# Turning q and k by crossbar DMA transposes instead of PE transposes, in a fused attention and SwiGLU kernel

## The chip, the cores and the metric

One core of a Trainium2 chip. The metric is the time of one execution on the device in microseconds (us), lower is better.

The engines are named as in the profile: PE (TensorE, matmuls), PEld (its weight loads), DVE (VectorE), ACT (ScalarE), POOL (GpSimd), SP (the sync queue, which only issues DMAs). PSUM is the memory that matmuls write to.

## The reference

Eight batches of attention with eight heads, 576 positions and head size 64, with a decay from f; its output (4608 tokens of 512) is normalised and goes through a SwiGLU layer of width 1536.

```python
scores = q @ k.T / sqrt(64) + cum[:, None] - cum[None, :]   # cum = cumsum(log f), causal
x   = softmax(scores) @ v                                   # 4608 x 512 over all heads
xn  = x / sqrt(mean(x * x) + 1e-6) * rms_g
out = (silu(xn @ w_gate) * (xn @ w_val)) @ w_out
```

## The kernel before

All is in bf16 on PE. The kernel emits attention of batch 0, then interleaves the attention of the batches 1 to 7 with the feed-forward work of nine output groups of 512 tokens. A scheduler of the framework sets the final order of instructions on each engine, and each engine works through its own list in order.

```python
qb = [ldp.tile([128, NB, H * D], BF16, name=f"qb{i}") for i in range(2)]   # two buffers
kb = [ldp.tile([128, NB, H * D], BF16, name=f"kb{i}") for i in range(2)]
Vs = [ldp.tile([128, NB, H, D + 1], BF16, name=f"Vs{i}") for i in range(2)]
def load_qk(b):                                   # POOL issues, casts to bf16
    for j in range(NB):
        for src, dst in ((q, qb[b % 2]), (k, kb[b % 2])):
            nc.gpsimd.dma_start(out=dst[0:n, j, :]..., in_=src[b, :, p0:p0 + n, :]...)
def load_v(b):                                    # the sync queue issues
    ...  nc.sync.dma_start(out=v32[0:n, :, :], in_=v[b, ...]...)
# ... weights are loaded in pieces by POOL ...
def scale_v(b):                                   # "Vs": POOL, ten instructions a batch
    for j in range(NB):
        nc.gpsimd.tensor_tensor(Vs[b % 2][0:n, j, :, 0:D], v32[0:n, :, :], bcast(dj, D), ALU.mult)
        nc.gpsimd.tensor_copy(Vs[b % 2][0:n, j, :, D], dj)
def transposes(b, p):                             # four head pairs p
    for src, store, nm in ((qb[b % 2], QT, "QT"), (kb[b % 2], KT, "KT")):
        tp = ps_tr.tile([128, NB * 128], BF16, name="tr")
        for j in range(NB):
            nc.tensor.transpose(tp[:, j * 128:(j + 1) * 128], src[:, j, p * 128:(p + 1) * 128], ident)
        t = store[b, p] = qkt.tile([128, NB * 128], BF16, name=f"{nm}{p}")
        nc.vector.tensor_copy(t, tp)
# scores (PE, exp on ACT, causal mask on POOL), values (PE, scaled on DVE) ...
def norm(b):
    ...                                           # squares on ACT
    nc.gpsimd.tensor_scalar(ms, in0=sq, ...)      # POOL
    nc.gpsimd.tensor_tensor(rs, ms, mhalf, ALU.pow)
    for j in range(NB):
        nc.vector.tensor_scalar_mul(xn[:, j, :], x[:, j, :], rs[:, j:j + 1])   # DVE
# transpose_x(b): PE turns xn for the feed-forward part ...
for i in range(3): load_w(i)
load_qk(1); load_v(1); load_wo()
for _, work in attention(0): work()
for b in range(1, B):
    stream.append((0.0, lambda b=b: (load_qk(b + 1), load_v(b + 1)) if b + 1 < B else None))
    stream += attention(b)        # transposes, last score rows and scale_v, scores, values, norm, transpose_x
# ... stream is dealt out between the pieces of the feed-forward work ...
```

POOL issues the q and k loads, scales v (Vs), masks the scores, and makes rs, the factor of the norm.

The softmax here doesn't subtract the row's maximum and nothing guards it: scores larger than these inputs give would overflow.

Of the kernel before, what the change touches and what calls it, by code (L numbers as in the profile page):

```python
# [9 lines left out]
BF16 = mybir.dt.bfloat16  # L10
# [13 lines left out]
def kernel(  # L24
# [12 lines left out]
    nc = tc.nc  # L37
    B, H, S, D = q.shape
    assert (B, H, S, D) == (8, 8, 576, 64)
    BH = B * H  # L40
    NB = 5
# [9 lines left out]
    ldp = ctx.enter_context(tc.tile_pool(name="ldp", bufs=1))  # L51
    vp = ctx.enter_context(tc.tile_pool(name="vp", bufs=6))
    qkt = ctx.enter_context(tc.tile_pool(name="qkt", bufs=2))
# [7 lines left out]
    ps_tr = ctx.enter_context(tc.tile_pool(name="ps_tr", bufs=1, space=PSUM))  # L61
# [5 lines left out]
    qb = [ldp.tile([128, NB, H * D], BF16, name=f"qb{i}") for i in range(2)]  # L67
    kb = [ldp.tile([128, NB, H * D], BF16, name=f"kb{i}") for i in range(2)]
    Vs = [ldp.tile([128, NB, H, D + 1], BF16, name=f"Vs{i}") for i in range(2)]
    PT4 = [[ldp.tile([128, 5 * 64], BF16, name=f"PT4_{i}{j}") for j in range(2)] for i in range(2)]  # L70


    def load_qk(b):
        for j in range(NB):
            p0, n = j * 128, min(128, S - j * 128)
            for src, dst in ((q, qb[b % 2]), (k, kb[b % 2])):
                nc.gpsimd.dma_start(  # L77
                    out=dst[0:n, j, :].rearrange("p (h d) -> p h d", d=D),
                    in_=src[b, :, p0:p0 + n, :].rearrange("h p d -> p h d"))
# [10 lines left out]
    fr = consts.tile([BH, S], F32)  # L90
    nc.sync.dma_start(out=fr, in_=f.rearrange("b h s -> (b h) s"))

    for t in qb + kb:
        nc.vector.memset(t[64:128, NB - 1, :], 0.0)
    load_qk(0)
    load_v(0)
    for t in Vs:
        nc.vector.memset(t[64:128, NB - 1, :, :], 0.0)
    for pair in PT4:
        for t in pair:  # L100
# [4 lines left out]
    ident = consts.tile([128, 128], BF16)  # L105
# [46 lines left out]
    QT, KT, PT = {}, {}, {}  # L152
# [8 lines left out]
            nc.gpsimd.tensor_copy(Vs[b % 2][0:n, j, :, D], dj)  # L161

    def transposes(b, p):
        for src, store, nm in ((qb[b % 2], QT, "QT"), (kb[b % 2], KT, "KT")):
            tp = ps_tr.tile([128, NB * 128], BF16, name="tr")
            for j in range(NB):
                nc.tensor.transpose(tp[:, j * 128:(j + 1) * 128], src[:, j, p * 128:(p + 1) * 128], ident)  # L167
            t = store[b, p] = qkt.tile([128, NB * 128], BF16, name=f"{nm}{p}")
            nc.vector.tensor_copy(t, tp)

    def scores4(b):

        for par in range(2):
            sc = ps_sc.tile([128, 512], F32, name="sc")
            rows = slice(par * 64, par * 64 + 64)
            for p in range(4):
                nc.tensor.matmul(sc[:, p * 64:(p + 1) * 64], lhsT=KT[b, p][rows, 512:640],
                                 rhs=QT[b, p][rows, 512:576], start=True, stop=True)
            t = PT4[b % 2][par]
            nc.scalar.activation(t[:, 0:256], sc[:, 0:256], ACT.Exp, scale=scale)  # L180
# [35 lines left out]
    def weights_of(b, h, qi, kj):  # L216
        if qi == 4:
            if kj == 4:
                c = (h // 2) * 64
                return PT4[b % 2][h % 2][:, c:c + 128]  # L220
            return PT[b, h][:, 1024 + kj * 64:1024 + kj * 64 + 128]
# [47 lines left out]
    def attention(b):  # L269

        a = []
        for p in range(4):
            a.append((0.6, lambda p=p: transposes(b, p)))
        a.append((0.2, lambda: (scores4(b), scale_v(b))))
        for p in range(4):
            for bank in range(3):
                a.append((0.35, lambda p=p, bank=bank: scores(b, p, bank)))
                if p > 0 and bank > 0:
                    a.append((0.45, lambda h=2 * (p - 1) + bank - 1: values(b, h)))
        a.append((0.45, lambda: values(b, 6)))  # L280
        a.append((0.45, lambda: values(b, 7)))
        a.append((0.0, lambda: norm(b)))
        for dc in range(NDC):
            a.append((0.3, lambda dc=dc: transpose_x(b, dc)))
        return a
# [53 lines left out]
    done_a, i, n = 0.0, 0, 0  # L339
# [40 lines left out]
```

## Time and profile before

486.84 us, median of two runs (486.47 to 487.2). The profiled execution spans 484.0 us.

From the page of the kernel before: the busy time of each engine, and the span in 40 equal slices of 12.1 us (a digit is a share in tenths, 9 is 90% or more; PEclk is the clock granted to PE; DMA is the mean share of the 16 DMA engines; in the tables of windows it adds up the times of all packets, which overlap, so it can exceed 1).

```profile
span 484.0 us, 8505 instructions
...
PE 423.9 (88%) x3317; PEld 207.6 (43%) x3317; DVE 260.3 (54%) x534; ACT 222.1 (46%) x436; POOL 187.7 (39%) x335
...
PE   0491707999999999999999999999999999999996
...
PEclk9999999999999999999999999999999999999999
DMA  9999991594190419041903290010001000201102
```

From the eighth slice on PE is busy 90% or more of every slice but the last. Before that it mostly is not, and in the first six of those slices the DMA engines are full. The table of windows says the same of two stretches, the start and one batch in the middle (busy us and number of instructions by engine, the granted clock, the DMA share and rate):

```profile
core 0: us, PE busy (x) PEld busy (x) DVE busy (x) ACT busy (x) POOL busy (x), PEclk, DMA share, GB/s
0.00:72.00 72.00, 28.03 (x237) 15.67 (x237) 15.75 (x47) 21.26 (x40) 56.13 (x94) 1.00 1.51 180
192.00:240.00 48.00, 46.83 (x398) 22.97 (x396) 29.49 (x62) 26.02 (x52) 22.60 (x40) 1.00 0.57 73
```

A batch in the middle takes 48.0 us, PE is busy 46.83 of them, so PE sets the pace there. The timeline of PE shows how a batch hands over to the next (start, duration, engine, line, operation; in brackets the idle time before and what ended it):

```profile
214.21 0.23 PE L258 MATMUL tr<-ident,xn 128*128 128x128 bf16 x1 [0.96 <-DVE xn L252]
...
220.85 0.44 PE L167 MATMUL tr<-ident,qb_100 128*128 128x128 bf16 x5
221.12 0.81 PE L311 MATMUL ff<-wo,hT 128*128 128x512 bf16 x3
```

PE waits 0.96 us for the normalised x. Line 167 is the transposes that the change takes away, here of the next batch, between matmuls of the feed-forward part. Each group of five covers 0.44 us.

The rs of norm 0 begins at 70.09 us.

### The profile page before, as it was taken

The page shows a single profiled execution, that of the slowest core. Times are in us where ns is not written, and L with a number is a line of the kernel's source. Part 1 is how long each engine was busy: PE and PEld are TensorE (multiplying, and loading weights), DVE is VectorE, ACT ScalarE, POOL GpSimd, SP SyncE. Part 2 cuts the span into 40 slices and gives each one's busy share as a digit, 9 for nine tenths or more (in the row PEclk, how much of TensorE's full clock was granted, in tenths as well). Part 3 has the DMA queues.
Part 4 walks back from the last instruction along what each step waited for, and adds up shares of the span by engine and source line. Part 5 has one row for each costly group of instructions (what it writes and reads, how often), then busy time and mean ns, then how long its engine had stood idle before and what let it go on. Part 6 is the DMA issues. An engine that isn't in the chain of part 4 may idle for free.

```text
span 484.0 us, 8505 instructions
## 1 busy us (share of the span) xinstructions
PE 423.9 (88%) x3317; PEld 207.6 (43%) x3317; DVE 260.3 (54%) x534; ACT 222.1 (46%) x436; POOL 187.7 (39%) x335
## 2 busy tenths in 40 slices
PE   0491707999999999999999999999999999999996
PEld 0231403454544454445444544454444544444442
DVE  3210326478447844784478457745774577373670
ACT  3060321664465437544754474447444744232321
POOL 8539990665182518252825282513111211000000
PEclk9999999999999999999999999999999999999999
DMA  9999991594190419041903290010001000201102
GB/s 151 175 195 178 191 187 33 36 65 99 65 120 3 100 66 119 3 100 67 120 1 77 70 118 0 1 66 23 3 0 66 23 1 0 88 1 45 43 1 87
DMA packets 123080, 33.73 MB, mean 70 GB/s; under 512 B 113760, under 2 KB 118368, under 8 KB 123040
## 3 DMA queue, kind: packets, MB, share of 16 engines
q0 software_dynamic: 79744, 14.16, 36.6%
q1 hardware_dynamic: 43296, 19.03, 14.9%
q8 instruction: 26, 0.43, 0.4%
q14 instruction: 14, 0.11, 0.1%
HBM read 37.90 MB, written 9.44 MB: 98 GB/s over the span
## 4 chain that ended last, share of the span: by engine, by line
PE 67%; POOL 13%; issue 6%; DMA 6%; ACT 5%; DVE 2%; POOLq 0%; ACTq 0%
PE ff L311 20%; PE ff L296 14%; PE ff L304 13%; PE sc L202 7%; PE po L231 5%; PE tr L167 4%; DMA wv<-in_moe_w_val_dram 3%; PE tr L258 3%; POOL Vs_104 L160 2%; DMA qb_100<-in_q_dram 2%; ACT junk L245 2%; POOL Vs_105 L160 2%; POOL rs L249 2%; ACT PT L205 2%; POOL qb_100 L77 2%
## 5 line engine op out<-in xcount | busy, mean ns | idle before, releaser
L205 ACT ACTIVATE PT<-sc 128x512 bf16<-128x512 f32 x192 | 105.1, 599 | 87.6 <-PE sc L202 73.8
L296 PE MATMUL ff<-xT,wg 128*128 128x512 bf16 x432 | 114.7, 382 | 0.7 <-DVE xT L265 0.6
L304 PE MATMUL ff<-xT,wv 128*128 128x512 bf16 x432 | 114.0, 380 | 0.0
L311 PE MATMUL ff<-wo,hT 128*128 128x512 bf16 x432 | 112.5, 380 | 0.0
L301 DVE SCALAR_TENSOR_TENSOR ga<-th,ff 128x512 f32<-128x512 f32 x108 | 74.2, 687 | 66.9 <-ACT th L299 66.3
L299 ACT ACTIVATE th<-ff 128x512 f32<-128x512 f32 x108 | 64.5, 598 | 82.6 <-PE ff L296 80.9
L306 DVE SCALAR_TENSOR_TENSOR hT<-ga,ff 128x512 bf16<-128x512 f32 x108 | 74.2, 687 | 9.0 <-PE ff L304 0.3
L304 PEld LDWEIGHTS <-wv 128*128 128x128 bf16 x432 | 42.2, 98 | 50.2 <-issue 2.5
L208 POOL TENSOR_SCALAR_AFFINE_SELECT PT<-PT 128x128 bf16<-128x128 bf16 x64 | 19.1, 299 | 97.8 <-ACT PT L205 97.6
L296 PEld LDWEIGHTS <-wg 128*128 128x128 bf16 x432 | 38.6, 98 | 42.0 <-issue 5.6
L314 ACT COPY ores<-ff 128x512 f32<-128x512 f32 x36 | 21.1, 586 | 75.2 <-PE ff L311 74.4
L213 POOL TENSOR_SCALAR_AFFINE_SELECT PT<-PT 128x384 bf16<-128x384 bf16 x64 | 33.0, 528 | 53.2 <-ACT PT L205 53.1
L311 PEld LDWEIGHTS <-hT 128*128 128x128 bf16 x432 | 36.5, 98 | 36.4 <-issue 9.5
L231 PEld LDWEIGHTS <-PT 128*128 128x128 bf16 x896 | 35.7, 102 | 31.2 <-POOL PT L208 9.7
L234 DVE RECIPROCAL rden<-po 128x5 f32<-128x5 f32 x64 | 12.2, 191 | 55.3 <-PE po L231 55.3
L258 PE MATMUL tr<-ident,xn 128*128 128x128 bf16 x160 | 20.6, 229 | 18.3 <-DVE xn L252 18.0
L231 PE MATMUL po<-Vs_104,PT 128*128 128x65 bf16 x448 | 22.7, 206 | 13.6 <-POOL PT L208 9.2
L235 DVE TENSOR_TENSOR x<-po,rden 128x320 f32<-128x320 f32 x64 | 31.4, 490 | 1.7
L245 ACT ACTIVATE junk<-x 128x512 bf16<-128x512 f32 x40 | 25.0, 624 | 9.0 <-DVE x L235 8.4
L258 PEld LDWEIGHTS <-xn 128*128 128x128 bf16 x160 | 12.4, 100 | 37.0 <-DVE xn L252 29.1
L265 DVE TENSOR_SCALAR xT<-tr,rg 128x512 bf16<-128x512 bf16 (+7 forms) x64 | 20.5, 362 | 12.3 <-PE tr L258 12.1
L252 DVE TENSOR_SCALAR xn<-x,rs 128x512 bf16<-128x512 f32 x40 | 18.1, 520 | 13.2 <-POOL rs L249 13.2
(300 smaller groups left out, 387.8 us busy)
## 6 DMA issues: line engine op xcount, KB each, us to landing
out_dram<-ores SPq DMA_DIRECT2D x36, 256.0 KB, 2.0
qb_100<-in_q_dram POOLq DMA_DIRECT2D x16, 128.0 KB, 5.3
kb_102<-in_k_dram POOLq DMA_DIRECT2D x16, 128.0 KB, 5.4
qb_101<-in_q_dram POOLq DMA_DIRECT2D x16, 128.0 KB, 4.4
kb_103<-in_k_dram POOLq DMA_DIRECT2D x16, 128.0 KB, 4.5
wg<-in_moe_w_gate_dram POOLq DMA_DIRECT2D x3, 512.0 KB, 12.7
wv<-in_moe_w_val_dram POOLq DMA_DIRECT2D x3, 512.0 KB, 14.0
wo<-in_moe_w_out_dram POOLq DMA_DIRECT2D x2, 768.0 KB, 12.3
```

The costliest lines, as they stand in the source:

```text
L202: nc.tensor.matmul(sc[:, c:c + n], lhsT=KT[b, p][rows, kj * 128:(kj + 1) * 128], rhs=QT[b, p][rows, q0:q0 + n], start=True, stop=True)
L205: nc.scalar.activation(t[:, bank * 512:(bank + 1) * 512], sc, ACT.Exp, scale=scale)
L213: nc.gpsimd.affine_select(out=d, in_=d, pattern=[[0, 3], [1, 128]], compare_op=ALU.is_ge, fill=0.0, base=0, channel_multiplier=-1)
L231: nc.tensor.matmul(po[:, qi, :], lhsT=weights_of(b, h, qi, kj), rhs=Vs[b % 2][:, kj, h, :], start=(kj == 0), stop=(kj == qi))
L245: nc.scalar.activation(junk, x[:, j, :], ACT.Square, accum_out=sq[:, j:j + 1])
L258: nc.tensor.transpose(tp[:, j * 128:(j + 1) * 128], xn[:, j, dc * 128:(dc + 1) * 128], ident)
L296: nc.tensor.matmul(pg, lhsT=wg[:, dc, fc * 128:(fc + 1) * 128], rhs=xT[:, dc, :], start=(dc == 0), stop=(dc == NDC - 1))
L299: nc.scalar.activation(t, pg, ACT.Tanh, scale=0.5)
L301: nc.vector.scalar_tensor_tensor(a, in0=t, scalar=1.0, in1=pg, op0=ALU.add, op1=ALU.mult)
L304: nc.tensor.matmul(pv, lhsT=wv[:, dc, fc * 128:(fc + 1) * 128], rhs=xT[:, dc, :], start=(dc == 0), stop=(dc == NDC - 1))
L306: nc.vector.scalar_tensor_tensor(hTs[g][:, fc, :], in0=a, scalar=0.5, in1=pv, op0=ALU.mult, op1=ALU.mult)
L311: nc.tensor.matmul(po, lhsT=hTs[g][:, fc, j * 128:(j + 1) * 128], rhs=wo[:, fc, :], start=(fc == 0), stop=(fc == NFC - 1))
```

## The change

The intent is to take 320 transposes with their weight loads off PE, the engine that sets the pace, and 64 copies out of PSUM off DVE. Ten DMA transposes a batch, from SBUF to SBUF on the sync queue, turn whole rows of heads (128 x 512, the last one 64 x 512).

```diff
+    QTs = [ldp.tile([128, 4, NB * 128], BF16, name=f"QTs{i}") for i in range(2)]
+    KTs = [ldp.tile([128, 4, NB * 128], BF16, name=f"KTs{i}") for i in range(2)]
 ...
-    for t in qb + kb:
-        nc.vector.memset(t[64:128, NB - 1, :], 0.0)
+    for t in QTs + KTs:
+        nc.vector.memset(t[:, :, S:], 0.0)
 ...
     def transposes(b, p):
-        for src, store, nm in ((qb[b % 2], QT, "QT"), (kb[b % 2], KT, "KT")):
-            tp = ps_tr.tile([128, NB * 128], BF16, name="tr")
+        if p > 0:
+            return
+        for src, store, ts in ((qb[b % 2], QT, QTs), (kb[b % 2], KT, KTs)):
+            t = ts[b % 2]
             for j in range(NB):
-                nc.tensor.transpose(tp[:, j * 128:(j + 1) * 128], src[:, j, p * 128:(p + 1) * 128], ident)
-            t = store[b, p] = qkt.tile([128, NB * 128], BF16, name=f"{nm}{p}")
-            nc.vector.tensor_copy(t, tp)
+                n = min(128, S - j * 128)
+                nc.sync.dma_start_transpose(out=t[:, :, j * 128:j * 128 + n], in_=src[0:n, j, :])
+            for pp in range(4):
+                store[b, pp] = t[:, pp, :]
```

## The prediction

> **What bounds the kernel now.** The page gives a span of 484.0 us with PE busy 423.9 (88%). Busy time by stages: from 144 to 384 us every 48.0 us are one batch, PE busy 46.8 of them, DVE 29.5, ACT 26.0, DMA share 0.5 falling to 0.06. There PE's in-order stream is the bound. From 0 to 72 us it is not: PE is busy 28 us, the DMA share is above 1 at 155 to 191 GB/s, and the chain of waits runs through q/k loads, weight loads and POOL (Vs scaling from 40.4, norm at 70).
>
> **What goes.** 320 PE transposes with weight loads, and 64 DVE copies of 128x640 out of PSUM (492 ns each, 31 us, DVE not the bound). In the timeline five pipelined transposes show as 0.44 us but push PE's next matmul back only 0.27 to 0.37. Eight groups a batch: 2.2 to 3.0 us; over the seven batches after the first, 15 to 21 us. The chain of waits agrees (line 167: 3.6% of the span, 17.4 us). All of it is on the critical path.
>
> **What comes.** 80 crossbar transposes of 128x512 (64x512) bf16 on the sync queue, ten a batch[...]. The trace has no such operation. The Trainium skill (VectorE: DVE Perf Modes, The three transpose paths) gives 1309 ns for 128x128 by DMA; four blocks in series would be 5.2 us. Its page DMA: Bandwidth & Descriptors (Latency and other measured facts) has 261 GB/s for one kernel, 0.5 us per 128 KB. My estimate lies between: 1 to 2.5 us each in throughput, 3 to 5 us to landing. Ten are 10 to 25 us of DMA per 45 us of PE: it fits beside a share of 0.5.
>
> **Is it on the path?** By the order of instructions the sync queue takes the transposes of a batch well ahead of its scores (those of batch 4 stand after the first output group, their scores two groups later), so in steady state a landing of 10 us is hidden. Stores and v loads share the queue but have slack. Expected: 45.0 to 45.8 us a batch.
>
> The start differs. The first ten transposes wait for q and k (last near 19.5 us), then issue into saturated DMA engines, where sync issues took 2.2 us each and v loads 6 to 10 us to land. First scores move from 22.7 to about 30 to 36 us. Much is hidden, since values wait for POOL's Vs (46 us) anyway; but weight loads and POOL's queue slip. Against that, the new order lets PE do much of batch 1's scores and values before the first norm, in its idle stretch from 60 to 72. I net these at -4 to +12 us.
>
> **Prediction:** 486.8 - 18 - 1 = about 468 us, 8 in 10 between 454 and 498. Chances: faster 0.62, same 0.22, slower 0.16.
>
> **Signs.** Right: a batch period of 45 to 46 us with PE 97% busy; median landing of a transpose under 6 us; no wait of scores on a DMA after 100 us; first scores near 33 us. Wrong at the start: first scores after 40 us, norm of batch 0 after 80. Wrong in steady state: scores waiting on transposes, or sync-queue waits in front of v loads.
>
> **What would make it wrong.** Transposes at 5 us or more in throughput: ten take 50 us, more than a batch, and the time goes beyond 500. Transposes that block other queues, so that loads and stores land late. ACT's exp and PSUM buffers taking over where the transposes were. A start that loses over 15 us cancels the gain.

## More of the kernel before

POOL's timeline shows how the norms get there in time, the first at the start and one in the middle:

```profile
70.09 1.21 POOL L249 TENSOR_TENSOR rs<-ms,mhalf 128x5 f32<-128x5 f32 x1
...
206.00 1.05 POOL L160 TENSOR_TENSOR Vs_105<-v_2632,decT 128x512 bf16<-128x512 f32 x1 [3.20 <-PE po L231]
...
212.43 1.20 POOL L249 TENSOR_TENSOR rs<-ms,mhalf 128x5 f32<-128x5 f32 x1
```

In the middle POOL has scaled the v of the next batch from 206.00 on, well before the norm at 212.43, and nothing else stands between. The q and k loads that follow this norm stand ahead of the next Vs in POOL's list (issued from 228.01 to 240.05 us, Vs from 254.03), but they are done 14 us before it.

## The result

The changed kernel takes 512.77 us (median; 511.44 to 514.11), 5.4% more: ratio 1.054, 95% interval 1.0466 to 1.0613. Ratios here and below are not quite the ratios of the medians. The median of the kernel before was 486.13 to 486.84 us in all sessions, which ran on several chips.

The page of the changed kernel, the same lines (slices of 12.8 us):

```profile
span 512.2 us, 7970 instructions
...
PE 401.5 (78%) x2997; PEld 192.0 (37%) x2997; DVE 230.6 (45%) x470; ACT 216.8 (42%) x436; POOL 188.2 (37%) x335
...
PE   0002848367599974999199999999999999999997
...
PEclk9999999999699995999789999999999999999999
DMA  9999999989961598219911252031100100100102
```

PE does 22.4 us less work, as intended, and the span is 28.2 us longer, so PE is idle 50.6 us more. The row of PE shows where: an emptier start, a 7 and a 4 in the slices fifteen and sixteen, and a 1 in slice twenty, where before there were only nines. The granted clock falls in the last two of these as well. By windows (the start; the hole in the middle; a batch late in the kernel; columns as above):

```profile
0.00:72.00 72.00, 16.35 (x143) 7.87 (x145) 8.37 (x30) 17.29 (x30) 44.56 (x73) 1.00 1.66 166
188.00:199.00 11.00, 0.34 (x2) 0.00 (x0) 0.05 (x1) 0.03 (x1) 10.81 (x17) 0.61 1.18 152
262.00:306.00 44.00, 42.77 (x356) 20.32 (x355) 25.49 (x53) 24.93 (x52) 14.01 (x30) 1.00 0.31 73
```

At the start PE does 16.35 us of work where it did 28.03. From 188 to 199 us it stands still while POOL is busy all the time. Late, a batch takes 44.3 us, 3.7 less than before. PE's timeline at these places:

```profile
47.37 0.32 PE L182 MATMUL sc<-QTs,KTs 64*128 64x64 bf16 x3 [47.37 <-DMA KTs<-kb]
...
106.37 0.34 PE L182 MATMUL sc<-QTs,KTs 64*128 64x64 bf16 x3 [10.20 <-DMA KTs<-kb]
...
187.31 1.02 PE L309 MATMUL ff<-xT,wv 128*128 128x512 bf16 x4
199.55 0.29 PE L263 MATMUL tr<-ident,xn 128*128 128x128 bf16 x1 [11.21 <-DVE xn L257]
```

The first scores wait for transposed k until 47.37 us (22.7 before), and those at 106.37 wait 10.20 us for k once more. At 199.55 PE has waited 11.21 us for xn, where it waited 0.96 before. The first matmul of 128 x 512 after that shows 0.63 us instead of 0.38: after the idle stretch the granted clock is low. The Trainium skill (TensorE: Matmul & The Clock Gate, Part 1: The HAM clock gate) says that PE falls to half its clock after an idle window of about 3.4 us. This trace agrees as to the half: the mean granted clock is 1.00 from 188.4 to 190.4 us and 0.50 from 190.5 to 204.0. It was halved some 2 us after PE's last matmul, which ended at 188.33, so sooner than after 3.4 idle us.

POOL's timeline, of the first norm and of the one that PE waits for at 199.55:

```profile
79.80 1.05 POOL L162 TENSOR_TENSOR Vs<-v,decT 128x512 bf16<-128x512 f32 x1 [2.21 <-DMA v<-in_v_dram]
...
90.86 1.23 POOL L254 TENSOR_TENSOR rs<-ms,mhalf 128x5 f32<-128x5 f32 x1
...
173.87 0.90 POOL L79 DMA_DIRECT2D qb<-in_q_dram  x1 [1.38 <-DMA QTs<-qb]
...
180.36 0.89 POOL L79 DMA_DIRECT2D kb<-in_k_dram  x1 [2.46 <-DMA QTs<-qb]
...
187.51 1.75 POOL L79 DMA_DIRECT2D kb<-in_k_dram  x2 [5.37 <-DMA KTs<-kb]
189.26 1.06 POOL L162 TENSOR_TENSOR Vs<-v,decT 128x512 bf16<-128x512 f32 x1
...
197.78 1.20 POOL L254 TENSOR_TENSOR rs<-ms,mhalf 128x5 f32<-128x5 f32 x1
```

Line 79 is the issue of a q or k load, a DMA_DIRECT2D. In the middle these issues stop POOL: they may not overwrite qb and kb before the transposes have read them ("<-DMA QTs<-qb", "<-DMA KTs<-kb"). Vs, begun at 206.00 us before the norm at 212.43 in the kernel before, now starts only when the issues are done, at 189.26, and rs of the norm comes at 197.78, behind all of Vs and three more issues (194.92 to 197.42). So the loads stood ahead of Vs before the change too; what is new is that they are held until just before Vs and the norm are due. The sync queue's own timeline and its list of waits (total us, times, longest us, from 160 to 185 us) show why the transposes read so late:

```profile
11.10 13.83 SPq L172 DMA_TRANSPOSE QTs<-qb  x5
25.02 14.02 SPq L172 DMA_TRANSPOSE KTs<-kb  x5
...
171.01 2.50 SPq L172 DMA_TRANSPOSE QTs<-qb  x2
...
181.45 3.91 SPq L172 DMA_TRANSPOSE KTs<-kb  x3
...
SPq L172 <- PE sc L207: 10.5, 1, 10.5
```

The transposes of this batch begin at 171.01 us, because they write QTs and KTs, and the list of waits has the first of them wait 10.5 us for the last scores (line 207) that read those buffers. One issue takes 1.2 to 1.3 us there. At the start it takes 2.8 us on average (13.83 us for five). The list of DMA issues, of the first 50 us and of the stretch from 140 to 300 us (number, median us from issue to landing):

```profile
QTs<-qb SPq DMA_TRANSPOSE x7, 11.2
KTs<-kb SPq DMA_TRANSPOSE x6, 12.4
...
QTs<-qb SPq DMA_TRANSPOSE x15, 2.4
KTs<-kb SPq DMA_TRANSPOSE x14, 3.0
```

At the start a transpose lands after 11 to 12 us, later after 2.4 to 3.0 us.

Where the 28.2 us come from, by the times at which ACT copies the first piece of each output group out of PSUM:

| stretch | before, us | after, us | difference |
|---|---|---|---|
| start to norm 0 (rs on POOL) | 70.1 | 90.9 | +20.8 |
| norm 0 to first output group | 51.3 | 59.7 | +8.4 |
| group 0 to 1 | 48.7 | 55.0 | +6.3 |
| group 1 to 2 | 48.0 | 55.6 | +7.6 |
| group 2 to 6, four intervals | 192.0 | 177.2 | -14.8 |
| group 6 to the end | 73.8 | 73.8 | 0 |

The saving is real, 3.7 us a batch. It comes only after the second interval. The three gaps of PE for norms, 8.14 us at 133.62 (there PE waits for DVE, and DVE has waited 7.23 us for rs), 11.21 us at 199.55 and 10.97 us at 256.05, are in the second, third and fourth row. The last two follow loads that waited for transposes. Before the first, POOL issues ten loads from 116.16 to 125.5 us and then Vs, with rs at 130.33, and none of these issues waits for a transpose: there their own 0.7 to 0.95 us each keep the norm back. The gaps end when there is nothing left to load: the last q and k loads are issued at about 253 us.

### The profile page after: what moved, and what is told of

Read it like the earlier page. It is cut to its first block, busy times and chain, and to the rows that moved or that the text cites. A ratio compares the mean times of both kernels' runs of the same rounds, so it can differ in the third digit from the quotient of the medians. Undisturbed runs are those within 1.5% of the kernel's fastest.

```text
span 512.2 us, 7970 instructions
## 1 busy us (share of the span) xinstructions
PE 401.5 (78%) x2997; PEld 192.0 (37%) x2997; DVE 230.6 (45%) x470; ACT 216.8 (42%) x436; POOL 188.2 (37%) x335
## 4 chain that ended last, share of the span: by engine, by line
PE 54%; POOL 18%; DMA 15%; issue 7%; SPq 3%; ACT 2%; DVE 1%; POOLq 0%; ACTq 0%
PE ff L316 19%; PE ff L309 12%; PE ff L301 12%; DMA qb<-in_q_dram 9%; POOL Vs L162 6%; PE sc L207 5%; PE po L236 4%; POOL qb L79 3%; DMA KTs<-kb 3%; POOL kb L79 2%; PE tr L263 2%; DMA v<-in_v_dram 2%; SPq L172 2%; POOL rs L254 2%; POOL PT L218 2%
## 5 line engine op out<-in xcount | busy, mean ns | idle before, releaser
L316 PE MATMUL ff<-wo,hT 128*128 128x512 bf16 x432 | 106.9, 388 | 0.0
L207 PE MATMUL sc<-QTs,KTs 64*128 64x64 bf16 (+4 forms) x512 | 57.6, 270 | 4.7 <-ACT PT L210 3.6
L316 PEld LDWEIGHTS <-hT 128*128 128x128 bf16 x432 | 40.0, 100 | 42.4 <-issue 4.3
L182 PE MATMUL sc<-QTs,KTs 64*128 64x64 bf16 x64 | 3.4, 207 | 63.6 <-DMA KTs<-kb 63.6
L185 ACT ACTIVATE PT<-sc 128x256 bf16<-128x256 f32 x16 | 5.4, 382 | 107.8 <-PE sc L182 107.8
L236 PEld LDWEIGHTS <-PT 128*128 128x128 bf16 x960 | 39.8, 105 | 21.7 <-issue 6.4
L236 PE MATMUL po<-Vs,PT 128*128 128x65 bf16 x960 | 46.1, 205 | 2.3 <-DVE x L240 1.1
L162 POOL TENSOR_TENSOR Vs<-v,decT 128x512 bf16<-128x512 f32 (+1 forms) x40 | 41.8, 1046 | 9.6 <-PE po L236 6.4
L263 PE MATMUL tr<-ident,xn 128*128 128x128 bf16 x160 | 21.4, 235 | 28.2 <-DVE xn L257 28.2
L79 POOL DMA_DIRECT2D qb<-in_q_dram x40 | 35.0, 875 | 18.9 <-DMA QTs<-qb 7.7
L79 POOL DMA_DIRECT2D kb<-in_k_dram x40 | 34.4, 862 | 19.6 <-DMA KTs<-kb 9.3
```

What stands on the lines that cost most here:

```text
L79: nc.gpsimd.dma_start(out=dst[0:n, j, :].rearrange("p (h d) -> p h d", d=D), in_=src[b, :, p0:p0 + n, :].rearrange("h p d -> p h d"))
L207: nc.tensor.matmul(sc[:, c:c + n], lhsT=KT[b, p][rows, kj * 128:(kj + 1) * 128], rhs=QT[b, p][rows, q0:q0 + n], start=True, stop=True)
L236: nc.tensor.matmul(po[:, qi, :], lhsT=weights_of(b, h, qi, kj), rhs=Vs[b % 2][:, kj, h, :], start=(kj == 0), stop=(kj == qi))
L316: nc.tensor.matmul(po, lhsT=hTs[g][:, fc, j * 128:(j + 1) * 128], rhs=wo[:, fc, :], start=(fc == 0), stop=(fc == NFC - 1))
```

## The experiments

The theory has two parts. At the start, the transposes wait in full DMA engines, and what hangs on the sync queue and on POOL behind them comes late. In the middle, POOL's list puts loads that wait for transposes in front of Vs and the norm. The rivals are that DMA bandwidth taken by the transposes slows everything, and that two buffers for q and k are too few, so that a third would cure it.

All runs gave outputs within the tolerance; what that is worth is said under "none" and "verify". Every kernel was timed in 3 or 5 rounds, except "verify". The columns are rs of norm 0, the first output group, the next four intervals between groups (all from the profiles), the median time and the ratio with its interval.

| run | norm 0 | group 0 | intervals | us | ratio |
|---|---|---|---|---|---|
| before | 70.1 | 121.4 | 48.7 48.0 48.0 48.0 | 486.84 | 1 |
| after | 90.9 | 150.6 | 55.0 55.6 44.3 44.3 | 512.77 | 1.054 (1.0466 to 1.0613) |
| none | 75.3 | 126.5 | 41.7 44.3 44.3 44.3 | 464.23 | 0.9551 (0.9528 to 0.9573) |
| ordr | 98.4 | 141.7 | 43.4 45.0 45.0 44.3 | 481.77 | 0.9907 (0.9871 to 0.9942) |
| pe2 | 75.7 | 140.8 | 57.8 56.0 44.3 44.3 | 508.0 | 1.0462 (1.0429 to 1.0495) |
| pe2ordr | 74.4 | 127.0 | 45.2 45.0 45.0 44.3 | 470.67 | 0.9672 (0.9644 to 0.97) |
| qk3 | 91.2 | 151.7 | 55.3 44.3 44.4 44.3 | 505.29 | 1.0404 (1.0368 to 1.0439) |
| pe1ordr | 85.7 | 129.0 | 43.4 45.0 45.0 44.3 | 472.56 | 0.9714 (0.9661 to 0.9767) |
| ordrlate | 95.6 | 140.3 | 43.4 45.0 45.0 44.3 | 481.32 | 0.9894 (0.9859 to 0.993) |
| beforelate | 70.2 | 121.7 | 48.7 48.0 48.0 48.0 | 486.4 | 1.0005 (0.9983 to 1.0027) |
| ordrv | 85.7 | 131.8 | 48.1 47.4 47.6 47.7 | 490.66 | 1.0105 (1.008 to 1.013) |
| pe1ordrv | 77.2 | 122.0 | 48.9 46.6 47.8 47.8 | 480.91 | 0.9887 (0.9869 to 0.9905) |
| pe2ordrv | 66.8 | 122.4 | 47.8 47.8 47.8 47.8 | 481.75 | 0.9911 (0.9892 to 0.993) |
| beforev | 68.1 | 123.5 | 51.6 51.1 51.1 51.2 | 502.91 | 1.0335 (1.0314 to 1.0357) |
| ordrv1 | 87.0 | 130.1 | 45.2 45.0 45.0 44.3 | 474.39 | 0.9747 (0.9717 to 0.9776) |
| pe2ordrv1 | 67.8 | 121.3 | 45.2 45.0 45.0 44.3 | 464.92 | 0.9553 (0.9541 to 0.9566) |
| beforev1 | 67.5 | 119.6 | 47.6 48.0 48.0 48.0 | 484.03 | 0.9951 (0.9937 to 0.9966) |
| beforevx | 68.7 | 124.1 | 54.0 54.2 54.4 54.5 | 526.56 | 1.0836 (1.081 to 1.0863) |
| best2 | 67.6 | 119.5 | 44.5 44.4 44.3 44.3 | 462.4 | 0.9511 (0.9487 to 0.9535) |

The names are built from parts: "ordr" moves loads in POOL's list, "pe1" and "pe2" give the first one or two batches back to PE, "late" moves weight loads, "v" and "v1" move Vs.

### none: no transposes at all

A wrong kernel: QTs and KTs stay zero.

```diff
-        nc.vector.memset(t[:, :, S:], 0.0)
+        nc.vector.memset(t, 0.0)
-                nc.sync.dma_start_transpose(out=t[:, :, j * 128:j * 128 + n], in_=src[0:n, j, :])
+                pass
```

> The changed kernel with the 80 crossbar transposes left out altogether (QTs and KTs are only zeroed, the result is wrong on purpose). It is the bound: PE and DVE freed of the transposes, nothing put in their place. My theory (the PE transposes were worth about 2.7 us a batch on the critical path, and all of the loss comes from what the DMA transposes make wait) expects 460 to 472 us and about 45.2 us a batch in the steady stage. The rival that the removed PE work was not worth what I said (another engine or PSUM takes over) expects 478 us or more.

464.23 us, as expected, and 44.3 us a batch. This is what the change could save if the new transposes cost nothing and POOL's order stayed as it is; norm 0 comes at 75.3 us here, so a better order can still go below it. It also passed the comparison with the reference, because with inputs of this size the scores are near 0.01 and hardly change the result. So a correct result says nothing about the transposes; "verify" was made for that.

### ordr: the loads behind the norm

In this and the following kernels `tc.issue_after(x)` places what is issued inside it behind the instruction x of the same engine. Same bytes, same buffers, only POOL's order is changed.

```diff
-        nc.gpsimd.tensor_tensor(rs, ms, mhalf, ALU.pow)
+        rs_of[b] = nc.gpsimd.tensor_tensor(rs, ms, mhalf, ALU.pow).ins
+    def loads(b):
+        if b - 3 in rs_of:
+            with tc.issue_after(rs_of[b - 3]):
+                load_qk(b)
+        else:
+            load_qk(b)
+        load_v(b)
-        stream.append((0.0, lambda b=b: (load_qk(b + 1), load_v(b + 1)) if b + 1 < B else None))
+        stream.append((0.0, lambda b=b: loads(b + 1) if b + 1 < B else None))
```

> Changed kernel, with one thing altered: each batch's q/k loads are put on POOL's queue after the norm (rs) of three batches before, so that POOL's norm no longer stands behind a load that waits for a transpose to finish reading its buffer. Same transposes, same buffers, same start. Theory: the two PE gaps of 11 us (188 to 199 and 245 to 256 us) vanish, the start stays as late (first scores near 47 us), so 488 to 494 us. Rival (the DMA engines are simply too loaded, the gaps are bandwidth): the gaps stay and the time stays within 5 us of 512.8.

481.77 us, 31 us less than the changed kernel and better than the expected range. The gaps of 8 to 11 us are gone. POOL's timeline of this kernel, at the first norm and in the middle:

```profile
95.00 1.05 POOL L162 TENSOR_TENSOR Vs<-v,decT 128x512 bf16<-128x512 f32 x1 [6.61 <-DMA v<-in_v_dram]
...
98.41 1.20 POOL L255 TENSOR_TENSOR rs<-ms,mhalf 128x5 f32<-128x5 f32 x1
...
176.69 1.04 POOL L162 TENSOR_TENSOR Vs<-v,decT 64x512 bf16<-64x512 f32 x1
...
178.56 1.20 POOL L255 TENSOR_TENSOR rs<-ms,mhalf 128x5 f32<-128x5 f32 x1
179.72 1.06 POOL L79 DMA_DIRECT2D qb<-in_q_dram  x1
```

In the middle, Vs (ending at 177.7) and the norm at 178.56 now go ahead, and the loads follow at 179.72. Order alone did it, so bandwidth was not what held the middle, since the transposes move the same bytes. At the start the norm is later still, 98.41: POOL stands 6.61 us in front of Vs of a later batch, waiting for v, and the norm of batch 0 stands behind that.

### pe2 and pe2ordr: the first two batches back on PE

```diff
     def transposes(b, p):
+        if b < 2:        # "pe1": b < 1
+            for src, store, ts in ((qb[b % 2], QT, QTs), (kb[b % 2], KT, KTs)):
+                tp = ps_tr.tile([128, NB * 128], BF16, name="tr")
+                ...      # five PE transposes into tp, as before
+                t = store[b, p] = ts[b % 2][:, p, :]
+                nc.vector.tensor_copy(t, tp)
+            return
```

> Changed kernel, but batches 0 and 1 are transposed on PE as before (into the same QTs and KTs), batches 2 to 7 by DMA. Theory: the start comes back (first scores near 23 us, first output group near 120 us in place of 148), the two later gaps of about 11 us stay, so 482 to 490 us. Rival (the start is not the transposes' doing, or the loss is spread over all batches in proportion to their number): 500 us or more.

508.0 us: the expectation was missed, and the time lies where the rival had put it. Yet the start did come back, with first scores at 22.75 us and norm 0 at 75.7, but group 0 came only at 140.8 us. Norm 1 came no earlier than in the changed kernel (132.3 us for 130.3), although norm 0 had come 15.2 us earlier: POOL's list held it, and PE has the same three gaps (7.47 us at 134.11, 11.53 at 191.88, 11.1 at 249.09). Of the 15.2 us 9.8 arrived at group 0, and the next two intervals gave back 3.2 of them. The two losses do not simply add.

> Both repairs at once: PE transposes for batches 0 and 1, and q/k loads behind the norm on POOL. Theory: losses add up and both are gone, what stays is the gain of six batches at 2.2 to 3 us: 468 to 474 us, faster than the kernel before. Rival (transposes by DMA cost as much in steady state as they save): 484 us or more.

470.67 us, as expected. Both parts of the theory are needed, and together they leave 6.4 us to "none".

### qk3: a third buffer for q and k

```diff
-    xp = ctx.enter_context(tc.tile_pool(name="xp", bufs=2))
+    xp = ctx.enter_context(tc.tile_pool(name="xp", bufs=1))      # for room
-    qb = [... for i in range(2)]        # kb alike, and b % 2 becomes b % 3
+    qb = [... for i in range(3)]
```

> Changed kernel with three q and k buffers in place of two (x has one buffer in place of two to make room). Each load then waits for the transposes of three batches before. If two buffers were the cause as such, the gaps go and the time falls to about 482, as it did when only the order was changed. My theory says it is the order on POOL: the instruction order puts the loads still one batch further ahead, again directly behind transposes that have not run, so at least one norm stays held for about 11 us, and only the last held norm goes because the loads run out one batch sooner: 492 to 508 us.

505.29 us, as expected. One of three gaps went, two stayed (17.75 us at 144.66, 10.47 us at 201.33). A third buffer does not free the norm from standing behind loads: during the longer gap POOL again issues loads and works on Vs, and rs begins at 142.86. The run also has one buffer of x less, and what that costs was not tested apart.

### pe1ordr, ordrlate and its control beforelate: what of the start costs

"pe1ordr" gives only batch 0 back to PE. "ordrlate" keeps all DMA transposes and moves the weight loads behind those of batch 1; "beforelate" does that to the kernel before.

```diff
-    for i in range(3):
-        load_w(i)
     load_qk(1)
     load_v(1)
+    for i in range(3):
+        load_w(i)
```

> Loads behind the norm, PE transposes for batch 0 alone; batch 1 by DMA, in the middle of the weight loads. Splits the 11 us between the two earlier runs (481.8 with both by DMA, 470.7 with both on PE). Theory: the first batch carries most of it because its scores start the chain: 470 to 475 us. If batch 1 (last of its transposes landed near 72 us) carries it: 477 to 482 us.

472.56 us, as expected: batch 0 carries nearly all that the first two batches cost, 9.2 of 11.1 us. The four runs lie between 469.51 and 474.73, so the rest is within the noise.

> All batches by DMA, loads behind the norm, and the gate and value weights are loaded after q, k, v of batch 1 in place of before. Theory (at the start the transposes are slow only because the DMA engines are full of weights: 2.8 us an issue and 11 us to landing, against 1.2 and 2.3 us later): first scores at 28 to 38 us in place of 45.6, and 470 to 478 us in place of 481.8. Rival (the start is slow because sync issues ten in a row whatever else runs): first scores still after 42 us, time within 3 us of 481.8.

The first scores came at 36.7 us instead of 45.6, as expected, but the time stayed at 481.32: missed. So earlier first scores alone win nothing while norm 0 is held elsewhere: it hardly moved (95.6 after 98.4), and that was the clue for the next series.

> Control: the kernel before, with the same later weight loads and nothing else. If the later weights help by themselves, it falls below 484; I expect 482 to 490 us, because its first scores did not wait for weights.

486.4 us, the same as before, as expected.

### ordrv, pe1ordrv, pe2ordrv and their control beforev: Vs behind every norm

In "ordr" norm 0 waited on POOL behind Vs of the batches 1 and 2, whose v loads stood behind transposes on the sync queue. This series puts Vs of batch b behind the norm of batch b - 1.

```diff
+    def scale_v_behind(b):
+        if b > 0:
+            with tc.issue_after(rs_of[b - 1]):
+                scale_v(b)
+        else:
+            scale_v(b)
-        a.append((0.2, lambda: (scores4(b), scale_v(b))))
+        a.append((0.2, lambda: (scores4(b), scale_v_behind(b))))
```

> All batches by DMA, q/k loads behind the norm as in the run that gave 481.8, and now also each batch's scaling of V (Vs) put on POOL behind the norm of the batch before. At the start that takes norm 0 out from behind Vs of batches 1 and 2, whose v loads stand on the sync queue behind transposes. New theory of the start (not late first scores but norm 0, at 98 us in that run, held by v loads behind transposes): norm 0 at 80 to 88 us, first output group near 128, time 468 to 475 us. Rival (the saturated DMA engines set the start): norm 0 after 92, time within 3 us of 481.8.

Norm 0 came 12.7 us earlier and group 0 9.9 us earlier, as expected. But every later batch took 47.4 to 48.1 us instead of 43.4 to 45.0, and the time was 490.66: missed.

> The same order, batch 0 transposed on PE. If norm 0 is what sets the start, this is at most 3 us better than the all-DMA version with the same order: 466 to 472 us.

480.91 us: missed for the same reason.

> The same order, batches 0 and 1 transposed on PE; a candidate for the best version. It was 470.7 with Vs unordered; norm 0 was already at 74 us there, so at most 3 us are left: 466 to 471 us.

481.75 us: missed alike.

> Control: the kernel before with only the Vs-behind-norm order (no loads order, no DMA transposes). Its norm 0 stood at 70 us behind Vs work; at most 3 us to win: 482 to 487 us. If it falls below 478, the best versions owe their gain to the order and not to the transposes.

502.91 us, 51.1 us a batch: missed, and useful, since this kernel has no DMA transpose at all. What costs 3.1 us a batch is thus Vs behind the norm, not the transposes. The trace of "beforev" shows what happens there, first DVE, then POOL and then PE after one norm:

```profile
218.62 4.42 DVE L253 TENSOR_SCALAR xn<-x,rs 128x512 bf16<-128x512 f32 x5 [0.70 <-POOL rs L250]
```

```profile
217.39 1.20 POOL L250 TENSOR_TENSOR rs<-ms,mhalf 128x5 f32<-128x5 f32 x1
218.57 1.03 POOL L160 TENSOR_TENSOR Vs<-v,decT 128x512 bf16<-128x512 f32 x1
...
219.91 1.28 POOL L160 TENSOR_TENSOR Vs<-v,decT 128x512 bf16<-128x512 f32 x1
```

```profile
219.95 0.23 PE L259 MATMUL tr<-ident,xn 128*128 128x128 bf16 x1 [1.74 <-DVE xn L253]
...
221.53 0.29 PE L259 MATMUL tr<-ident,xn 128*128 128x128 bf16 x1 [0.52 <-DVE xn L253]
```

DVE's five instructions for xn take 4.42 us beside Vs; in the kernel before they take 2.07. POOL's second and third Vs instructions are slower there too (1.28 us, where they take 1.04 alone; the first is not). PE waits 1.74 us for the first xn, where it waited 0.96, and 0.52 us for a later one. The table of windows for two stretches after that norm (the columns as before, the granted clock third from the end):

```profile
218.00:221.30 3.30, 1.27 (x6) 0.28 (x5) 2.68 (x3) 0.00 (x0) 3.30 (x5) 1.00 0.11 25
221.35:224.70 3.35, 3.17 (x10) 1.19 (x11) 3.35 (x7) 0.00 (x0) 3.35 (x6) 0.50 0.74 168
```

PE is busy only 1.27 of 3.30 us, and in the next 3.4 us it works at half its clock. An estimate from these numbers: 1.3 us of longer waits and half of the 3.17 us at half clock, 1.6 us, make 2.9 of the 3.1 us. The trace shows that the clock fell after PE had waited, not at what share of busy time it falls. The Trainium skill (SBUF — State Buffer, Who interferes with whom) says that DVE's instructions in a two-port mode, which a tensor_scalar can enter, and POOL's instructions exclude each other from a shared pair of ports. The trace agrees in kind: both slow down where they overlap. Whether xn runs in such a mode here is not shown.

### ordrv1, pe2ordrv1 and their control beforev1: only Vs of batches 1 and 2 behind norm 0

```diff
-        if b > 0:
-            with tc.issue_after(rs_of[b - 1]):
+        if b in (1, 2):
+            with tc.issue_after(rs_of[0]):
```

> All batches by DMA, loads behind the norm, Vs of batches 1 and 2 alone behind norm 0 (from batch 3 on as in the run that gave 481.8). The last run showed norm 0 at 86 us and the first output group 10 us earlier, but every later batch 3.4 us longer. If the start's loss is Vs held by v loads and the 3.4 us is Vs held behind every norm, both go: 469 to 475 us, batches at 44.3 to 45.2. If the start gains nothing for the end (the later stages lose it again): 479 or more.

474.39 us with norm 0 at 87.0, as expected. The first scores are as late as ever (47.3 us), and yet 7.4 us are won over "ordr": this part of the start's loss was the norm's place on POOL.

> The same with batches 0 and 1 transposed on PE. 470.7 without the Vs order, whose norm 0 stood 7.5 us later: 464 to 470 us, the best version.

464.92 us, as expected, and 0.7 us from "none".

> Control: the kernel before with Vs of batches 1 and 2 behind norm 0 and nothing else: 482 to 487 us. Below 478 the gain of the other two would be the order's, not the transposes'.

484.03 us, as expected: of the 21.9 us that "pe2ordrv1" is faster than before, about 3 are owed to the place of Vs, and about 19 to the DMA transposes together with the order of the loads. No run has that order alone in the kernel before; but group 0 comes at the same time (121.3 and 121.4 us), and the gain lies in the intervals of 44.3 to 45.2 us against 48.0 to 48.7, which "none" has too.

### beforevx and best2: what stands beside xn

Batches take 45.0 us where loads are issued right behind the norm, 44.3 where there are no more loads. Two runs test whether POOL's work beside xn explains this and the 3 us of the "v" series. "beforevx" puts Vs behind the masks of that batch's last score rows. "best2" is "pe2ordrv1" with the loads behind such masks.

```diff
+            sc4_of[b] = nc.gpsimd.affine_select(...).ins       # in scores4
# beforevx, against beforev
-            with tc.issue_after(rs_of[b - 1]):
+            with tc.issue_after(sc4_of[b]):
# best2, against pe2ordrv1
-            with tc.issue_after(rs_of[b - 3]):
+            with tc.issue_after(sc4_of[b - 2]):
```

> The kernel before with Vs of each batch behind the masks of that batch's last score rows, so later than in beforev (behind the norm) but no longer beside the five DVE instructions that make xn. If beforev lost its 3.1 us a batch because DVE's xn and POOL's Vs ran side by side (five xn took 4.43 us there, 2.07 before, and the granted clock fell to 0.97): xn back at 2.1 us, clock above 0.99, 48.0 us a batch, 484 to 489 us in all. If Vs came too late for the values: xn back, but PE waits before values and a batch still takes 50 to 52 us, 498 to 510 us.

526.56 us, 54 us a batch: the second reading in kind, but beyond its range (498 to 510 us). The xn instructions are back at 2.07 us, but Vs comes too late, and PE waits for it before the values in steps of up to 1.0 us, 17.7 us in all. So this run does not isolate the cost of Vs beside xn.

> pe2ordrv1 with the q and k loads behind the masks of a batch's last score rows instead of right behind the norm. If POOL's issue of loads beside xn is what makes a batch 45.0 us where no load follows it takes 44.3 (five xn 2.70 us beside issues, 2.07 without): xn near 2.1 us in all norms after the first, batches of 44.3 to 44.5 us, 462 to 464.3 us. If not: 45.0 us a batch and 464.5 to 466 us.

462.4 us, as expected. It is the fastest version: ratio 0.9511, 4.9% faster than the kernel before. It is also 1.8 us below "none", which does not have the better place of Vs (norm 0 at 67.6 us here, 75.3 there). In "pe2ordrv1" POOL and DVE show, after one norm:

```profile
204.96 1.20 POOL L265 TENSOR_TENSOR rs<-ms,mhalf 128x5 f32<-128x5 f32 x1
206.12 1.06 POOL L79 DMA_DIRECT2D qb<-in_q_dram  x1
```

```profile
206.19 2.69 DVE L268 TENSOR_SCALAR xn<-x,rs 128x512 bf16<-128x512 f32 x5 [0.70 <-POOL rs L265]
```

In "best2" DVE shows, after the same norm:

```profile
203.79 2.07 DVE L270 TENSOR_SCALAR xn<-x,rs 128x512 bf16<-128x512 f32 x5 [0.71 <-POOL rs L267]
```

The xn instructions take 2.07 us instead of 2.69, and the three intervals of 45.0 to 45.2 us fall to 44.3 to 44.5. Issuing loads on POOL beside xn did cost 0.6 to 0.7 us a batch.

### verify: are the DMA transposes right?

Since "none" passed too, this kernel (with the orders of "ordrv1") also turns every block on PE, takes the difference, and adds a million times the difference to QTs and KTs, so that any error would spoil the output.

```diff
+                nc.vector.tensor_tensor(d, tp, t, ALU.subtract)            # tp: by PE, t: by DMA
+                nc.vector.scalar_tensor_tensor(t, in0=d, scalar=1e6, in1=t, op0=ALU.mult, op1=ALU.add)
```

> Not a timing run. The run without any transposes was found correct, because scores of this input are about 0.01 and the tolerance does not see them; so correct says nothing about the transposes. Here all 80 DMA transposes of the order-mended version are compared on the chip with PE transposes of the same q and k, and a million times the difference is added to Q and K: any misplaced element makes scores that overflow and a wrong output. If the crossbar transposes are right, in the crowded start too, the result is correct; if any is corrupted, wrong or not finite. Time: slower than the kernel before, of no interest.

Correct, 515.23 us in one run (state unknown, and its time is of no use). That the comparison bites was seen in the check that runs before the chip: this kernel passes there, and it is refused for scores that are not finite when the DMA transposes are left out, and also when one of the 80 reads a wrong block.

## Why the prediction was wrong

The direction was wrong: 468 us with a range of 454 to 498 was predicted, 512.77 measured.

- **What goes: right, and a little too small.** "Eight groups a batch: 2.2 to 3.0 us." It is 3.7 us, 0.46 for each group of five transposes, by the intervals of 48.0 and 44.3 us in a stretch where PE sets the pace in both kernels. That PE was the bound was right.
- **What comes: right.** The estimate was 1 to 2.5 us each in throughput and 3 to 5 us to landing. Measured was 1.2 to 1.3 us an issue and 2.4 to 3.0 us to landing in the middle, 3.8 and 3.9 us as medians of all. The figure of the skill for 128 x 128 (1309 ns), taken four times in series, would have been far too high.
- **The step that failed:** "in steady state a landing of 10 us is hidden", with "Stores and v loads share the queue but have slack". The landing was hidden from the scores in the steady state, as said, but the scores were not all that waits for a transpose. A transpose may not overwrite QTs or KTs before the last scores have read them (10.5 us of waiting at 171.01), so the buffers qb and kb come free later, the loads for them stand in POOL's list, and behind these stand Vs and the norm, for which PE waits. PE lost 11.21 and 10.97 us so, and 8.14 us at the norm before, where the loads stood ahead of the norm without waiting for a transpose. "ordr" shows it: the same transposes with another order on POOL are 31 us faster, and the three gaps are gone. The prediction named sync-queue waits in front of v loads as a sign, and missed POOL's list. For the steady state it reasoned from the order of the sync queue alone, though the order of POOL's instructions could be read before the run as well.
- **The start: right in kind, wrong in size.** First scores were expected at 30 to 36 us and came at 47.4; the net was put at -4 to +12 us. To norm 0 it was +20.8 us, and to the first output group +29.2 with the first of the three gaps. The reason given, full DMA engines, was a part of it. The Trainium skill (DMA: Bandwidth & Descriptors, Issuing engines are not separate DMA queues) says that DMAs of all issuing engines share the same 16 engines; the trace agrees, with 2.8 us an issue and 11 to 12 us to landing there. The other part is again a place on POOL: norm 0 behind Vs of later batches, whose v loads stand behind transposes. "ordrlate" (first scores earlier by 9 us, nothing won) and "ordrv1" (first scores no earlier, 7.4 us won) tell the two apart. With both orders mended, giving the first two batches back to PE is worth another 9.5 us ("pe2ordrv1"). The prediction had named a loss of over 15 us at the start as what would cancel the gain, and that loss came about too.
- **The signs.** The landing held (under 6 us), and the batch period, once it came, was better than the sign (44.3 for 45 to 46). First scores after 40 us and norm 0 after 80 us were named as signs of a wrong start, and both occurred. No wait of scores on a DMA was to occur after 100 us; one did, 10.20 us at 106.37.

What stays open: the division of the 3.1 us a batch of Vs behind every norm (waits for xn, half clock) rests on one batch of one trace; the run that was to isolate it brought another wait. A third buffer for QTs and KTs, which would let the transposes read earlier without a change of order, was not tried. Between "ordrv1" and "pe2ordrv1" 9.5 us remain at the start, which go with the transposes of the batches 0 and 1 in full DMA engines; how much of it is slow transposes and how much is their place before the v loads was not divided.

## What to carry to other kernels

Work taken off the engine that sets the pace is won only where nothing new comes between it and that pace: ask of a new asynchronous step not only who reads its output, but what must be done before it may write, who waits until it has read its input, and what stands behind that waiter on its engine. In an in-order list, an issue that must wait for a buffer blocks all compute behind it, so put loads behind the small instruction that the critical engine needs next, and not beside DVE's work for it. Keep the old way for the first batches, where the DMA engines are full and PE is idle anyway.

## What the Trainium skill lacked or had wrong

- VectorE: DVE Perf Modes (The three transpose paths) gives 1309 ns for a 128 x 128 transpose by DMA. Here 128 x 512, four such blocks, was issued every 1.3 us and landed in 2.4 to 3.0 us where the DMA engines had room. The figure does not add up block by block, and the page does not say so.
- DMA: Bandwidth & Descriptors (Latency and other measured facts) has 261 GB/s for DMA_TRANSPOSE. From SBUF to SBUF on one queue, 128 KB (128 x 512 x 2 bytes) every 1.3 us are 101 GB/s; the issues stand back to back there. The page names no issue time for such a transpose on trn2 (1.2 us here, 2.8 us on average beside full DMA engines); cycle counts for earlier generations stand only in its part on a newer chip. It has no landing time in company (11 to 12 us).
- TensorE: Matmul & The Clock Gate (the table at its top) has POOL's queue as strict FIFO. No page that was read draws the consequence that cost most here: a DMA issue on POOL that waits for its buffer holds all of POOL's compute (11.21 and 10.97 us of idle PE).
- TensorE: Matmul & The Clock Gate (Part 1: The HAM clock gate) does not say at what busy share of a window the clock is halved. Here it was halved some 2 us after the last matmul in the changed kernel, and in "beforev" after 3.3 us in which PE was busy for 1.27.
- SBUF — State Buffer (Who interferes with whom) says that the loser of the shared ports fully blocks for one instruction, and gives no cost for a series. Here both sides were stretched: five xn instructions of DVE 4.42 us for 2.07 beside POOL's tensor_tensor, 2.69 beside POOL's issue of loads, and POOL's tensor_tensor 1.28 for 1.04.
